# Loads of one chunk moved to another queue, and the first five chunks ordered anew

## The chip, the cores and the metric

The kernel runs on one core of a Trainium2 chip. The metric is device time in microseconds, from runs of the whole program. Five engines work beside each other, each through its own list of instructions in program order: TensorE (PE, matmuls and transposes; its weight loads are listed as PEld), VectorE (DVE), ScalarE (ACT), GpSimd (POOL) and SyncE (SP). They wait for each other by semaphores. Sixteen DMA engines move data. Transfers are put into queues: here SP issues nearly all of them, and GpSimd those of the weights, which are converted from float32 to bfloat16 on the way.

## The reference

Two steps, with B = 4, H = 8 heads, S = 768 positions, D = 64. First attention in which each query sees the first four positions (the sink) and the 128 latest:

```python
scores = scale * np.matmul(q, k.transpose(0, 1, 3, 2))
is_sink = pos[None, :] < n_sink                    # n_sink = 4
rel = pos[:, None] - pos[None, :]
keep = is_sink | ((rel >= 0) & (rel < window))     # window = 128
a = softmax(np.where(keep, scores, -1e9))
attn = np.matmul(a, v)
```

Then its output, as x of 3072 tokens by 512, goes through a feed-forward layer whose hidden layer is the largest of three products:

```python
h = np.maximum(np.maximum(x @ w1, x @ w2), x @ w3)   # 512 x 768 each
out = h @ w_out                                       # 768 x 512
```

## The kernel before

The 3072 tokens are cut into 12 chunks of 256 (`NCH`), three to a batch (`CPB`). Chunks 0 to 5 use one layout, those from `NEW = 6` on another with smaller score tiles. Four pairs of heads (`p` 0 to 3) are worked on at a time; two 64-row heads share the 128 rows of TensorE. For a chunk `ci` the steps are these helpers:

- `load(ci, what)` (lines 93 to 110) issues from SP the DMAs of Q, K and V in float32, 512 KB each, or in two halves of four heads (`part`, 256 KB). A `gate` puts a tiny write into the target tile by GpSimd first, so that SP's DMA waits for GpSimd to get there: `pool_gate` a memset (L603), `after(wi, c)` a copy of one element of weight `wi` (L599), which also waits for that weight to have landed.
- `cast_qk(ci, w, g, eng)` (L118) turns half `g` of Q or K to bfloat16 on the engine named; `cast_v` (L123, or L129 from chunk 6 on) does so for V, `cast_k` (L90) for K from chunk 6 on.
- `turn(ci, w, g, eng)` and `turn2` transpose that half by four matmuls with an identity matrix (L138, L164) into PSUM, and the engine named copies it out (L142, L149, L168, L171). From chunk 4 on `turn_dma` (L182, L188) does it by a transposing DMA that SP issues.
- `premask(ci, pairs)` (L311) writes the additive mask into the score tile by a matmul; `score` (L331; L357 from chunk 6 on) adds the products; `expo` (L398, L374) is the exponential on ScalarE; where there was no `premask`, `mask` (L406, L389) multiplies by a 0/1 mask on VectorE.
- `sink_k(b)` (L283, GpSimd) and `sink_v(b)` (L437, L440) pick the sink's keys and values of batch `b`; `sink_score` (L423, L427) makes their scores.
- `av_open` (L453) takes four PSUM banks and puts the sink's part in; `av(ci, p)` (L471) multiplies with V. A column of ones in V gives the sums; VectorE takes their reciprocal (L476) and scales x by it (L479).
- `xpose(ci, t, eng)` (L491, L493) transposes x into `xT`; from chunk 4 on `xpose_dma` (L498).
- `ffn_h(ci, fp, wi)` (L517) makes 256 hidden columns (block `fp`) with weight `wi`: eight matmuls, then for `wi` 0 a copy by ScalarE (L523), for the others a maximum by VectorE (L527). `ffn_y` (L537) or `y_open`, `y_turn`, `y_out` (L561) make the output, `store` (L589) writes it.

The weights are loaded once, in thirds of 256 columns, by `load_w` (L292), the output weight by `load_wo` (L300), all from GpSimd.

The order of the work is written out by hand: `tc.manual_schedule()` keeps program order on each engine, and the places of the waits follow from the data. PSUM's eight banks are given out from a list, first freed, first taken (`bank`, `give`), when the program is built; so a step takes a fixed bank and waits for whatever used it last. Chunks 0 to 3, with the feed-forward work of chunks 0 to 2 between them, are one long list of calls (lines 629 to 835). A loop follows from `i = 3`: it makes the attention of chunk `i + 1`, the output of chunk `i - 1` and the hidden layer of chunk `i`. Its first turn (with the attention of chunk 4) and its last have an order of their own, the turns between them another.

Around the change the order before is: GpSimd issues the thirds of weight 0, then 1, then 2 (0, 1 and 2 as indices `wi`), while SP loads chunk 2's K and Q behind gates that open when the first weight is there, and its V behind a third gate:

```python
        load(2, 'k', part=0, parts=2, gate=after(0, 300))
        load(2, 'k', part=1, parts=2)
        ...
        load(2, 'q', part=1, parts=2)
        load(2, 'q', part=0, parts=2, gate=pool_gate)
        load_w(2, 0, 256)
        ...
        load(2, 'v', gate=after(0, 300))
```

Of the kernel before, what the change touches and what calls it, by code (L numbers as in the profile page):

```python
# [16 lines left out]
def kernel(  # L17
# [31 lines left out]
    with tc.manual_schedule():  # L49
# [43 lines left out]
        def load(ci, what="kqv", gate=None, part=None, parts=1):  # L93
# [4 lines left out]
            for w in what:  # L98
# [361 lines left out]
        def av(ci, p):  # L460
# [24 lines left out]
        def xpose(ci, t, eng=None):  # L485
# [8 lines left out]
            give(pt)  # L494

# [109 lines left out]
        def cast(ci):  # L605
            if ci >= NCH:
                return
            if ci == NEW:
                for g in range(2):
                    cast_qk(ci, "q", g, nc.gpsimd)  # L610
            for n in range(2):
                for h in range(2):
                    for i in range(2):
                        if ci >= NEW:
                            cast_k(ci, n, h, i, nc.gpsimd)
            if ci < NEW:
                for w in "kq":
                    for g in range(2):
                        cast_qk(ci, w, g, nc.gpsimd)
            if ci == NEW - 1:  # L620
                masks2()
# [6 lines left out]

        load(0, 'q', part=1, parts=2)
        warm(8)  # L630
# [3 lines left out]
        cast_qk(0, 'q', 1, nc.scalar)  # L634
        load(0, 'v', part=1, parts=2)
        masks()
        sink_init()
        factors(msk, addm)
        turn(0, 'q', 1, nc.scalar)
        warm(4)  # L640
        premask(0, (2,))
        cast_qk(0, 'k', 0, nc.scalar)
        cast_qk(0, 'k', 1, nc.vector)
        turn(0, 'k', 1, nc.vector)
        load(1, 'k')
        turn(0, 'k', 0, nc.scalar)
        cast_qk(0, 'q', 0, nc.gpsimd)
        premask(0, (3,))
        score(0, (2,))
        score(0, (3,))  # L650
        turn(0, 'q', 0, nc.vector)
        premask(0, (0,))
        load(1, 'q')
        expo(0, 2)
        cast_v(0, 1, 0, nc.gpsimd)
        cast_v(0, 0, 0, nc.vector)
        cast_v(0, 1, 1, nc.vector)
        cast_v(0, 0, 1, nc.vector)
        load_w(0, 512, 768)
        load(1, 'v')  # L660
        score(0, (0,))
        expo(0, 3)
        cast_qk(1, 'k', 0, nc.gpsimd)
        premask(0, (1,))
        score(0, (1,))
        expo(0, 0)
        expo(0, 1)
        load_w(0, 256, 512)
        av_open(0)
        av(0, 2)  # L670
        av(0, 3)
        turn2(1, 'k', 0, nc.vector)
        cast_qk(1, 'k', 1, nc.scalar)
        av(0, 0)
        cast_qk(1, 'q', 0, nc.gpsimd)
        cast_qk(1, 'q', 1, nc.scalar)
        turn(1, 'k', 1, nc.scalar)
        load_w(0, 0, 256)
        av(0, 1)
        premask(1, (0,))  # L680
        turn2(1, 'q', 0, nc.vector)
        sink_k(0)
        premask(1, (1,))
        turn(1, 'q', 1, nc.scalar)
        cast_v(1, 0, 0, nc.vector)
        cast_v(1, 1, 0, nc.vector)
        load_w(1, 512, 768)
        xpose(0, 0, nc.vector)
        score(1, (0,))
        score(1, (1,))  # L690
        expo(1, 0)
        expo(1, 1)
        load_w(1, 256, 512)
        cast_v(1, 1, 1, nc.gpsimd)
        xpose(0, 1, nc.vector)
        cast_v(1, 0, 1, nc.gpsimd)
        load_w(1, 0, 256)
        score(1, (3,))
        sink_score(1)
        load(2, 'k', part=0, parts=2, gate=after(0, 300))  # L700
        load(2, 'k', part=1, parts=2)
        sink_v(0)
        expo(1, 3)
        ffn_h(0, 2, 0, 1, nc.vector)
        score(1, (2,))
        load(2, 'q', part=1, parts=2)
        load(2, 'q', part=0, parts=2, gate=pool_gate)
        load_w(2, 0, 256)
        expo(1, 2)
        load_w(2, 256, 512)  # L710
        load_w(2, 512, 768)
        mask(1, 3)
        ffn_h(0, 1, 0)
        mask(1, 2)
# [288 lines left out]
```

## Time and profile before

| | |
|---|---|
| time, median of 3 runs | 176.2 us (176.18 to 177.06) |
| profiled execution | 176.05 us, its span 174.3 us |
| TensorE busy | 167.1 us of the span, 96% |
| VectorE, ScalarE, GpSimd busy | 124.6, 89.6, 110.5 us |
| DMA | 34.95 MB, 201 GB/s over the span |

The span runs from the first to the last instruction; the rest of the profiled execution's time lies around it. Rows of the profile read so: line, engine, operation, `target<-source` by the program's names, shapes, `xcount`; in a timeline a row begins with its start and its length in us, and brackets at its end give how long the engine had been idle and what ended that. `w<-in_moe_w_dram` is a weight's DMA, `q_raw`, `k_raw`, `v_raw` are the float32 tiles of Q, K and V. A transfer's time to landing is counted from the start of its issue. Since matmuls are pipelined, a row's length covers more than the time until the next one may start.

### The profile page before, as it was taken

The page shows a single profiled execution, that of the slowest core. Times are in us where ns is not written, and L with a number is a line of the kernel's source. Part 1 is how long each engine was busy: PE and PEld are TensorE (multiplying, and loading weights), DVE is VectorE, ACT ScalarE, POOL GpSimd, SP SyncE. Part 2 cuts the span into 40 slices and gives each one's busy share as a digit, 9 for nine tenths or more (in the row PEclk, how much of TensorE's full clock was granted, in tenths as well). Part 3 has the DMA queues.
Part 4 walks back from the last instruction along what each step waited for, and adds up shares of the span by engine and source line. Part 5 has one row for each costly group of instructions (what it writes and reads, how often), then busy time and mean ns, then how long its engine had stood idle before and what let it go on. Part 6 is the DMA issues. An engine that isn't in the chain of part 4 may idle for free.

```text
span 174.3 us, 5433 instructions
## 1 busy us (share of the span) xinstructions
PE 167.1 (96%) x2228; PEld 129.3 (74%) x2233; DVE 124.6 (71%) x262; ACT 89.6 (51%) x185; POOL 110.5 (63%) x193
## 2 busy tenths in 40 slices
PE   7979999999999999999999999999999999999992
PEld 2446879857696697697797797797797796896871
DVE  3387754796697895886886986877787876776452
ACT  4778535677954813916826617717636516510210
POOL 7399507546489999999999996989998700000000
PEclk9999999999999999999999999999999999999999
DMA  5999999999999999997999999999999415018303
GB/s 148 298 286 197 220 216 258 217 313 271 295 205 302 303 197 224 249 225 202 249 182 252 196 235 240 271 182 213 256 183 289 33 26 162 0 30 154 122 0 120
DMA packets 70505, 34.95 MB, mean 201 GB/s; under 512 B 26448, under 2 KB 68944, under 8 KB 70480
## 3 DMA queue, kind: packets, MB, share of 16 engines
q1 hardware_dynamic: 64784, 31.33, 81.7%
q0 software_dynamic: 5552, 3.15, 12.7%
q8 instruction: 17, 0.28, 0.7%
q10 hardware_dynamic: 144, 0.13, 0.2%
q14 instruction: 8, 0.07, 0.1%
HBM read 25.17 MB, written 6.29 MB: 180 GB/s over the span
## 4 chain that ended last, share of the span: by engine, by line
PE 68%; DMA 18%; POOL 7%; issue 2%; SPq 1%; ACT 1%; DVE 0%; POOLq 0%
PE h_ps L517 43%; PE y_ps L561 11%; DMA k_raw<-in_k_dram 4%; DMA q_raw<-in_q_dram 4%; PE o L471 4%; DMA w<-in_moe_w_dram 4%; PE y_ps L537 4%; PE st L357 3%; DMA v_raw<-in_v_dram 3%; DMA qT<-q_bf 3%; POOL vb L123 3%; POOL w L292 2%; SPq L107 1%; PE st L331 1%; POOL k_bf L118 1%
## 5 line engine op out<-in xcount | busy, mean ns | idle before, releaser
L517 PE MATMUL h_ps<-xT,w 128*128 128x256 bf16 x864 | 101.2, 273 | 0.6 <-DMA w<-in_moe_w_dram 0.4
L517 PEld LDWEIGHTS <-w 128*128 128x128 bf16 x864 | 81.8, 98 | 11.0 <-DMA w<-in_moe_w_dram 0.9
L527 DVE TENSOR_TENSOR h_sb<-h_sb,h_ps 128x512 bf16<-128x512 bf16 (+1 forms) x74 | 49.0, 670 | 17.8 <-PE h_ps L517 16.2
L523 ACT CAST h_sb<-h_ps 128x512 bf16<-128x512 f32 x35 | 20.6, 588 | 51.1 <-PE h_ps L517 51.0
L129 POOL CAST vb<-v_raw 32x512 bf16<-32x512 f32 x48 | 37.5, 781 | 4.0 <-DMA v_raw<-in_v_dram 1.3
L90 POOL CAST k_bf<-k_raw 32x512 bf16<-32x512 f32 x48 | 29.1, 607 | 2.4 <-POOL vb L129 0.4
L398 ACT ACTIVATE e_sb<-st 128x512 bf16<-128x512 f32 (+1 forms) x48 | 23.2, 591 | 1.1 <-PE st L331 1.1
L479 DVE TENSOR_TENSOR x_sb<-o,rc 128x256 bf16<-128x256 f32 x48 | 20.4, 424 | 1.7
L561 PE MATMUL y_ps<-wo,h_sb 64*64 64x512 bf16 (+1 forms) x312 | 21.1, 377 | 0.0
L471 PE MATMUL o<-vb,e_sb 128*128 128x65 bf16 x352 | 16.5, 193 | 0.8 <-DVE vb L123 0.8
L471 PEld LDWEIGHTS <-e_sb 128*128 128x128 bf16 x352 | 14.5, 97 | 3.1 <-ACT e_sb L398 1.0
L123 POOL CAST vb<-v_raw 64x512 bf16<-64x512 f32 x18 | 13.1, 729 | 5.1 <-DMA v_raw<-in_v_dram 4.6
L389 DVE TENSOR_TENSOR e_sb<-e_part,msk 128x1024 bf16<-128x1024 bf16 x16 | 13.4, 862 | 3.1 <-ACT e_part L374 3.0
L406 DVE TENSOR_TENSOR e_sb<-e_sb,msk 128x1024 bf16<-128x1024 bf16 (+1 forms) x18 | 13.1, 751 | 3.4 <-ACT e_sb L398 3.4
L561 PEld LDWEIGHTS <-h_sb 64*64 64x64 bf16 (+1 forms) x312 | 9.9, 106 | 5.0
L374 ACT ACTIVATE e_part<-st 128x384 bf16<-128x384 f32 x32 | 13.1, 496 | 0.5 <-PE st L357 0.5
L537 PE MATMUL y_ps<-wo,h_sb 128*128 128x512 bf16 x49 | 12.6, 380 | 0.3
L476 DVE RECIPROCAL rc<-o 128x4 f32<-128x4 f32 x48 | 8.4, 175 | 4.1 <-PE o L471 4.1
L118 POOL CAST k_bf<-k_raw 128x512 bf16<-128x512 f32 x6 | 3.8, 648 | 9.0 <-DMA k_raw<-in_k_dram 7.5
L118 ACT CAST q_bf<-q_raw 128x512 bf16<-128x512 f32 x13 | 7.6, 621 | 2.7 <-DMA q_raw<-in_q_dram 2.7
L537 PEld LDWEIGHTS <-h_sb 128*128 128x128 bf16 x54 | 4.9, 97 | 5.4 <-DVE h_sb L527 0.5
L427 ACT ACTIVATE e_sink<-sk 128x256 bf16<-128x256 f32 x8 | 3.1, 389 | 10.3 <-PE sk L423 10.3
(90 smaller groups left out, 143.7 us busy)
## 6 DMA issues: line engine op xcount, KB each, us to landing
k_raw<-in_k_dram SPq DMA_DIRECT2D x11, 512.0 KB, 5.8
v_raw<-in_v_dram SPq DMA_DIRECT2D x11, 512.0 KB, 6.7
out_dram<-y_sb SPq DMA_DIRECT2D x11, 512.0 KB, 3.7
q_raw<-in_q_dram SPq DMA_DIRECT2D x10, 512.0 KB, 7.4
w<-in_moe_w_dram POOLq DMA_DIRECT2D x9, 256.0 KB, 6.5
q_raw<-in_q_dram SPq DMA_DIRECT2D x4, 256.0 KB, 7.6
wo<-in_moe_w_out_dram POOLq DMA_DIRECT2D x2, 384.0 KB, 8.2
v_raw<-in_v_dram SPq DMA_DIRECT2D x2, 256.0 KB, 5.1
```

What stands on the lines that cost most here:

```text
L90: f(bfs[ci, "k"][x:x + 32, :, n], raws[ci, "k"][y:y + 32, :, i].rearrange("q (p a) d -> q p a d", a=2))
L123: eng.tensor_copy(vb[ci % RING][64 * i:64 * i + 64, n, :, 0:D], raws[ci, "v"][64 * n:64 * n + 64, :, i])
L129: eng.tensor_copy(vb[ci % RING][x:x + 32, n, :, 0:D], raws[ci, "v"][y:y + 32, :, i])
L389: nc.vector.tensor_mul(x.rearrange("q a (t s) c -> q (a t) s c", t=2), y, msk2)
L398: nc.scalar.activation(e[:, a, lo:], st[a][:, lo:], AF.Exp, scale=scale)
L471: nc.tensor.matmul(o[:, t, a], lhsT=e[:, a, s], rhs=vb[cv % RING][:, n, 2 * p + a], start=first, stop=True, skip_group_check=True)
L479: nc.vector.tensor_mul(xs[ci][:, p], o[:, :, :, 0:D], rc.unsqueeze(3).to_broadcast([128, 2, 2, D]))
L517: nc.tensor.matmul(hp[:, f].rearrange("q (i t r) -> q i t r", i=2, r=x.shape[3]), lhsT=w_sb[wi][:, ds, c0:c0 + 128], rhs=x, start=(ds == 0 ...
L523: (nc.scalar.copy if eng is nc.scalar else eng.tensor_copy)(dst, hp)
L527: nc.vector.tensor_max(dst[:, x], dst[:, x], hp[:, x])
L537: nc.tensor.matmul(yp, lhsT=hs[ci][:, fb, t * 128:(t + 1) * 128], rhs=wo[:, fb], start=(fb == 0), stop=(fb == FB - 1))
L561: nc.tensor.matmul(yps[ci][t][c:c + cols], lhsT=hs[ci][hp, fb, x:x + cols], rhs=wo[hp, fb], start=(turn == 0 and fb == 0), stop=(turn == 1 ...
```

## The change

The six 256 KB halves of chunk 2's Q, K and V are issued by GpSimd (`eng=nc.gpsimd`) and not by SP, without gates, in one queue with the weights: one half of Q behind the whole of weight 0, one half of K and both halves of V behind the whole of weight 1, the rest of Q and K between the thirds of weight 2. The output weight follows at once. Chunk 3's Q has `pool_gate` instead of a gate on weight 2.

The list of chunks 0 to 3 is put into another order, and chunk 4's attention, before the loop's first turn, becomes part of it. All twelve warming matmuls (`warm`) come before the first transposes. Some casts and copies change engines. The masks of chunk 1's pairs that are added beforehand are those of 1 and 2 rather than 0 and 1. `av` gets an engine: for `av(1, 3)`, `av(3, 0)` and `av(3, 1)` four ScalarE instructions do the scaling that was one of VectorE. A new `xpose2` makes both halves of chunk 1's `xT` with the transposes in turns. V of chunk 4 is loaded behind K and Q of chunk 5; of chunk 5's casts three go to ScalarE and one to VectorE. The middle turns of the loop issue what they did.

```diff
-        def load(ci, what="kqv", gate=None, part=None, parts=1):
+        def load(ci, what="kqv", gate=None, part=None, parts=1, eng=None):
...
-                    nc.sync.dma_start(
+                    (eng or nc.sync).dma_start(
...
-        def av(ci, p):
+        def av(ci, p, eng=None):
...
-            nc.vector.tensor_mul(xs[ci][:, p], o[:, :, :, 0:D],
-                                 rc.unsqueeze(3).to_broadcast([128, 2, 2, D]))
+            if eng is nc.scalar:
+                for t in range(2):
+                    for a in range(2):
+                        nc.scalar.activation(xs[ci][:, p, t, a], o[:, t, a, 0:D], AF.Copy,
+                                             scale=rc[:, t, a:a + 1])
+            else:
+                nc.vector.tensor_mul(xs[ci][:, p], o[:, :, :, 0:D],
+                                     rc.unsqueeze(3).to_broadcast([128, 2, 2, D]))
...
+        def xpose2(ci, eng0, eng1):
+
+            xTs[ci] = work.tile([128, DS, 2, 128], BF16, tag="xT", bufs=3, name="xT")
+            pt = [bank([128, DS, 128], BF16, "xt") for t in range(2)]
+            for ds in range(DS):
+                for t in range(2):
+                    nc.tensor.transpose(
+                        pt[t][:, ds], xs[ci][:, ds, t].rearrange("q a d -> q (a d)"), ident)
+            for t, eng in enumerate((eng0, eng1)):
+                (nc.scalar.copy if eng is nc.scalar else eng.tensor_copy)(xTs[ci][:, :, t], pt[t])
+                give(pt[t])
```

The new list, cut to what the prediction speaks of:

```python
        warm(4)
        masks()
        warm(8)
        load(0, 'q', part=1, parts=2)
        cast_qk(0, 'q', 1, nc.scalar)
        turn(0, 'q', 1, nc.scalar)
        premask(0, (2,))
        ...
        cast_qk(0, 'k', 1, nc.vector)
        factors(msk, addm)
        load(1, 'k')
        cast_qk(0, 'k', 0, nc.scalar)
        turn(0, 'k', 0, nc.vector)
        sink_init()
        turn(0, 'k', 1, nc.scalar)
        cast_qk(0, 'q', 0, nc.gpsimd)
        premask(0, (3,))
        turn(0, 'q', 0, nc.vector)
        premask(0, (0,))
        score(0, (2,))
        expo(0, 2)
        ...
        load_w(0, 256, 512)
        premask(1, (1,))
        load(1, 'v')
        load_w(0, 0, 256)
        ...
        load(2, 'q', part=0, parts=2, eng=nc.gpsimd)
        ...
        load_w(1, 512, 768)
        ...
        load_w(1, 256, 512)
        ...
        load_w(1, 0, 256)
        score(1, (3,))
        expo(1, 3)
        cast_v(1, 0, 1, nc.vector)
        load(2, 'k', part=0, parts=2, eng=nc.gpsimd)
        load(2, 'v', part=0, parts=2, eng=nc.gpsimd)
        load(2, 'v', part=1, parts=2, eng=nc.gpsimd)
        load_w(2, 0, 256)
        expo(1, 2)
        load(2, 'q', part=1, parts=2, eng=nc.gpsimd)
        load_w(2, 256, 512)
        load(2, 'k', part=1, parts=2, eng=nc.gpsimd)
        load_w(2, 512, 768)
        load_wo()
        mask(1, 3)
        ffn_h(0, 1, 0)
        av_open(1)
        av(1, 0)
        av(1, 1)
        ffn_h(0, 0, 0)
        av(1, 3, nc.scalar)
        av(1, 2)
        ffn_h(0, 2, 1)
        xpose2(1, nc.scalar, nc.vector)
        cast_qk(2, 'k', 0, nc.scalar)
        cast_qk(2, 'k', 1, nc.gpsimd)
        ffn_h(0, 1, 1)
        ffn_h(1, 0, 0)
        ffn_h(1, 0, 1)
        cast_qk(2, 'q', 0, nc.vector)
        factors(msk0[0], addm0)
        ffn_h(1, 2, 0)
        ffn_h(1, 2, 1)
        ffn_h(1, 1, 0)
        load(3, 'q', gate=pool_gate)
        cast_v(2, 1, 0, nc.gpsimd)
        ...
        turn(2, 'k', 0, nc.scalar)
        ...
        ffn_h(0, 0, 1)
        ffn_h(1, 1, 1)
        ffn_h(0, 0, 2)
        ffn_h(1, 1, 2)
        turn(2, 'q', 1, nc.scalar)
        turn(2, 'q', 0, nc.scalar)
        turn(2, 'k', 1, nc.scalar)
        ...
        ffn_y(0, 1)
        turn(3, 'q', 0, nc.scalar)
        av(2, 1)
        ...
        turn_dma(4, 'q')
        ...
        load(4, 'v')
        ...
        store(0)
        turn_dma(4, 'k')
        mask(3, 3)
        cast_v(4, 1, 0, nc.gpsimd)
        ...
        sink_k(1)
        sink_v(1)
        ...
        cast_qk(5, 'q', 1, nc.scalar)
        cast_qk(5, 'k', 1, nc.scalar)
        sink_score(4)
        store(1)
        turn_dma(5, 'k')
        ...
        store(2)
        av(4, 2)
        ...
        av(4, 0)
        turn_dma(5, 'q')
```

More of the change, by code (lines that the diff above doesn't have):

```diff
@@ L613, in cast @@
                     for i in range(2):
[L614 to L621, printed above, removed]
+                        cast_k(ci, n, h, i, nc.gpsimd)
             if ci > NEW and ci % CPB == 1:
@@ L633 @@
         load(0, 'v', part=0, parts=2, gate=pool_gate)
-        cast_qk(0, 'q', 1, nc.scalar)
         load(0, 'v', part=1, parts=2)
-        masks()
-        sink_init()
[L638 to L646, printed above, removed]
+        cast_qk(0, 'k', 1, nc.vector)
+        factors(msk, addm)
@@ L731 @@
[L731 to L739 removed]
+        ffn_h(1, 0, 0)
+        ffn_h(1, 0, 1)
+        cast_qk(2, 'q', 0, nc.vector)
+        factors(msk0[0], addm0)
+        ffn_h(1, 2, 0)
+        ffn_h(1, 2, 1)
+        ffn_h(1, 1, 0)
+        load(3, 'q', gate=pool_gate)
```

438 lines of the change are left out of this document (199 added, 239 removed).

## The prediction

> **What bounds the kernel now.** I read the windows first (columns: busy us and instruction count of each engine, granted clock, DMA share, GB/s), then the chain that ended last, then the waits of TensorE's weight loads.
>
> ```profile
> 20.00:25.00 5.00, 4.57 (x58) 4.03 (x54) 4.16 (x11) 0.69 (x2) 0.00 (x0) 1.00 1.32 229
> 25.00:30.00 5.00, 5.00 (x52) 4.53 (x51) 1.80 (x3) 3.38 (x6) 3.15 (x6) 1.00 1.27 242
> ...
> 70.00:80.00 10.00, 10.00 (x131) 8.22 (x128) 8.13 (x17) 5.83 (x13) 9.40 (x14) 1.00 0.82 206
> ```
>
> ```profile
> 16.47 6.56 DMA w<-in_moe_w_dram
> ...
> 23.08 3.67 PE h_ps L517 x32
> ...
> 63.38 4.85 DMA qT<-q_bf
> ...
> 68.28 0.29 PE sk L423 x4
> ...
> 76.99 4.37 PE h_ps L517 x40
> ```
>
> ```profile
> PEld L517 <- DMA w<-in_moe_w_dram: 0.6, 1, 0.6
> ...
> PEld L423 <- DMA qT<-q_bf: 0.3, 1, 0.3
> ```
>
> From 23.08 us TensorE is full: 5.00 of 5 us, later 10.00 of 10, at clock 1.00. So the end moves only by what TensorE gains or loses before 23.08 us, or by new holes behind it. Two holes show: 0.6 us of weight loads waiting for the last third of weight 1 (issued at 16.47, landed 23.03), and 0.3 us at 68.28 for chunk 5's transposed Q, of which some 0.1 is the normal step between two matmuls; I count 0.2. That is the whole prize: 0.8 us and crumbs. Eight matmuls of one `ffn_h` call take 4.37/5 = 0.87 us.
>
> What feeds the front is the DMA engines:
>
> ```profile
> 9.00:10.00 1.00, 0.42 (x5) 0.11 (x4) 0.99 (x2) 1.00 (x4) 1.00 (x2) 1.00 1.17 290
> ...
> 14.00:15.00 1.00, 1.00 (x22) 0.64 (x18) 0.99 (x3) 1.00 (x3) 1.00 (x2) 1.00 1.45 195
> ...
> 24.00:25.00 1.00, 1.00 (x12) 0.90 (x10) 0.69 (x1) 0.00 (x0) 0.00 (x0) 1.00 1.31 213
> ```
>
> They move 290 GB/s when only SP's Q, K, V are under way, 195 (counted in the bfloat16 written; twice that is read) when only GpSimd's weights are, 213 when both are. A weight third (256 KB written) alone thus costs 1.34 us of stream, a half of Q, K or V (256 KB) 0.90 us from SP. Over the span, in slices of 4.4 us:
>
> ```profile
> DMA  5999999999999999997999999999999415018303
> ```
>
> They are busy through the first 40 us, so what goes ahead of something delays it.
>
> **The change, part by part.**
>
> *Chunk 2 on GpSimd's queue.* Six halves of 256 KB leave SP and go into the one queue with the weights: q0 behind weight 0; k0, v0, v1 behind weight 1; q1 and k1 amid weight 2.
>
> ```profile
> 13.69 0.79 POOL L292 DMA_DIRECT2D w<-in_moe_w_dram  x1
> ```
>
> ```profile
> w<-in_moe_w_dram POOLq DMA_DIRECT2D x1, 256.0 KB, 6.0
> ```
>
> ```profile
> L292 POOL DMA_DIRECT2D w<-in_moe_w_dram x9: 740/747/1105, 9.3 to 18.9; - x9
> ```
>
> ```profile
> 17.25 0.18 POOL L599 CAST k_raw<-w 1x1 f32<-1x1 bf16 x1
> 17.37 0.09 POOL L603 MEMSET q_raw<- 1x1 f32 x1
> ...
> 26.70 0.61 POOL L118 CAST k_bf<-k_raw 128x512 bf16<-128x512 f32 x1 [6.91 <-DMA k_raw<-in_k_dram]
> ```
>
> Issuing: six times 0.75 us = 4.5 on GpSimd, against 0.4 for the three gates that go (two copies like the 0.18, one memset of 0.09). The 6.91 us in which GpSimd waited before 26.70 take all of it, and the two issues of the output weight now come ahead of the cast instead of behind it; without that idle time the 4.1 us would stand ahead of chunk 2's casts. SP loses five issues and waits for nothing of them. The Trainium skill ("SBUF — State Buffer", section "SBUF: two separate sides") speaks against the move: GpSimd cannot write descriptors while VectorE runs an operation that takes both ports. The nine issues of 740 to 1105 ns bear out 0.36 us at most, so 6 x 0.36 = 2.2 us would still go into the idle time.
>
> Transport: no transfer of plain float32 from GpSimd's queue is in this trace. Upper bound, a half at the weights' written rate: 1.34 us; lower bound, at their read rate (390 GB/s): 0.67. I take SP's 0.90, the same rows of 512 bytes. Weight 1's first third, issued at 13.69, landed 6.0 later at 19.7; with q0 ahead 20.6 (20.4 to 21.0). The second follows 1.34 later, at 21.9. The last third, landed 23.03 before with chunk 2's K on SP beside it, has only q0 ahead: about 23. From there the single queue gives k0 23.9, v0 24.8, v1 25.7, weight 2 first third 27.0, q1 27.9, second third 29.3, k1 30.2, last third 31.5, output weight about 36 (it shares with chunk 3's Q).
>
> *Chunks 0 and 1 anew.*
>
> ```profile
> 3.80 0.72 PE L203 MATMUL warm<-wz 128*128 128x512 bf16 x2
> 4.52 0.40 PE L138 MATMUL pt<-ident,q_bf 128*128 128x128 bf16 x4
> 4.76 0.59 PE L203 MATMUL warm<-wz 128*128 128x512 bf16 x2
> ```
>
> ```profile
> 4.96 0.58 ACT L142 COPY qT<-pt 128x512 bf16<-128x512 bf16 x1 [0.49 <-PE pt L138]
> 5.63 0.62 ACT L118 CAST k_bf<-k_raw 128x512 bf16<-128x512 f32 x1
> 6.77 0.58 ACT L149 COPY kT<-pt 128x512 bf16<-128x512 bf16 x1 [0.52 <-PE pt L138]
> 7.40 3.17 ACT L398 ACTIVATE e_sb<-st 128x384 bf16<-128x384 f32 x8
> ...
> 14.29 2.06 ACT L398 ACTIVATE e_sb<-st 128x512 bf16<-128x512 f32 x4
> 16.22 0.42 ACT L427 ACTIVATE e_sink<-sk 128x256 bf16<-128x256 f32 x1
> 16.48 2.12 ACT L398 ACTIVATE e_sb<-st 128x512 bf16<-128x512 f32 x4
> 18.39 0.69 ACT L523 CAST h_sb<-h_ps 128x512 bf16<-128x512 f32 x1
> ```
>
> ```profile
> 20.29 1.91 PE L517 MATMUL h_ps<-xT,w 128*128 128x256 bf16 x16
> ...
> 22.04 0.61 PE L491 MATMUL xt<-ident,x_sb 128*128 128x128 bf16 x8
> ```
>
> All twelve warming matmuls now stand ahead of the first transposes; the last four go at (0.59 - 0.38) = 0.21 each, so `turn(0,'q',1)` starts 0.7 late, near 5.2. ScalarE copies it at 5.65 to 6.23, and only then casts its half of K (5.63 before), behind which stand both transposes of K, since g = 0 now goes first: cast to 6.85, VectorE's copy to 7.8, ScalarE's to 8.1, first scores 8.25, first exponential 8.6 against 7.40, 1.2 us late. From there ScalarE's list sets the pace: eight exponentials at 3.17/8 = 0.40 to 11.8; copy of K, cast of Q, copy of K, first copy of xT (four of about 0.6, with 0.85 lost waiting for TensorE's banks and GpSimd's Q cast) to 15.0; then 4 x 0.51, 0.26 (16.22 to the next exponential at 16.48), 4 x 0.51 to 19.4; two casts of h to 20.85; and the scalings of `av(1,3)`, four of 128x64. For those no row exists: from 0.1 (the 128x512 start-to-start of 0.51 scaled by columns, no fixed part) to 0.4 (the 128x256 exponential); I take 0.2, being nearer to the 0.26 step. x is whole at 21.65 (21.25 to 22.5).
>
> TensorE meanwhile has the same matmuls. `av_open(1)` waits for `expo(1,3)`, to 18.5; then two `av`, `ffn_h(0,0,0)`, two `av` put `ffn_h(0,2,1)` at 20.55, where its weight lands at 20.6 (20.29 before). It ends 21.45; `xpose2` issues six transposes and waits 0.1 for the last scaling; `ffn_h(0,1,1)` runs 21.9 to 22.8 and covers the copies of xT. At 22.8 everything is done that before was done at 23.08, and the last third of weight 1 is first wanted one `ffn_h` later, at 23.7, when it has landed. Gain 0.3; bounds -0.5 (halves at 0.67, cheap scalings) to +0.7 (scalings 0.4, w late 0.4).
>
> *Chunk 2 and 3.* From 22.8 at 0.87 per call: `ffn_h(1,1,2)` is reached at 30.0 (weight 29.3), `turn(2,'k',1)` at 31.4 (k1 lands 30.2, GpSimd's cast 0.61 more: 30.9). Margins 0.7 and 0.5: no stall. The load of chunk 3's Q now stands behind that cast and two `factors` on GpSimd.
>
> ```profile
> 28.77 0.18 POOL L599 CAST q_raw<-w 1x1 f32<-1x1 bf16 x1
> 29.04 1.07 POOL L238 TENSOR_SCALAR msk<-addm 128x384 bf16<-128x384 bf16 x2
> ...
> 38.14 0.86 POOL L118 CAST q_bf<-q_raw 128x512 bf16<-128x512 f32 x1 [2.32 <-DMA q_raw<-in_q_dram]
> ```
>
> ```profile
> 39.93 0.39 PE L138 MATMUL pt<-ident,q_bf 128*128 128x128 bf16 x4
> ```
>
> Its gate opens at 30.9 + 1.07 = 32.0 instead of 28.95. The bytes ahead of it are the same and the engines have the output weight until then, so it still lands near 38 and is cast by 39.0. TensorE, 0.3 earlier, wants it one `av` (some 0.3) sooner than 39.93, at 39.3. SP's K and V of chunk 3 queue behind it and come no later either. If that cover is gone (output weight done before 32), every microsecond goes to chunk 3.
>
> *Chunks 3 and 4.* V of chunk 4 goes behind chunk 5's Q and K; GpSimd casts it only when landed, and `sink_k(1)` is queued behind that cast.
>
> ```profile
> 54.43 0.28 PE L423 MATMUL sk<-qT,ks 128*32 128x256 bf16 x4
> ```
>
> ```profile
> 45.97 3.45 SPq L182 DMA_TRANSPOSE kT<-k_bf  x2
> ```
>
> ```profile
> kT<-k_bf SPq DMA_TRANSPOSE x1, 5.5
> ```
>
> SP's queue behind Q 3 (through at 37) holds k3, v3, q4, k4, q5, k5 at 1.8 each, the transposed Q 4 (about 0.7) and V 4: it lands near 51, `sink_k(1)` is done 52.8, needed at 54.43 - 0.5 = 53.9. The transposing DMA of K 4 is issued near 47.2 rather than 45.97; 5.5 (first of two) on top is 52.7, the second about 53.6, needed 54. No stall, but half a microsecond to spare. Three casts of chunk 5 go from GpSimd to ScalarE, so `turn_dma(5,'q')` no longer waits for GpSimd's V casts: it is issued behind the store of chunk 2, near 60, and lands by 65, so the 0.2 at 68.28 goes. `av(3,0)` and `av(3,1)` on ScalarE (eight scalings, 1.6) lie beside `ffn_h`. The unrolled loop issues the same instructions.
>
> **Sum**: -0.3 - 0.2 = -0.5. Profiled execution 176.05 (span 174.3 and 1.75 around) gives 175.55; the median 176.2 is 0.15 higher, so I say **175.6**.
>
> **Rivals.**
>
> *A. Plain float32 on GpSimd's queue is slow (1.34 a half).* Ends slower. For it speaks that 195 GB/s is all this queue shows anywhere; against it, that each byte written there is two read. `ffn_h(0,2,1)` waits 0.45, k1 lands 6 x 0.44 = 2.6 later, so `turn(2,'k',1)` waits 1.7, and the output weight costs some 0.4 more: 175.55 + 2.5 = 178.0. It decides from 1.1 us a half.
>
> *B. ScalarE or an in-order queue is short.* Its list is full from 8.6 to 21.7; scalings at 0.4 and 0.3 of extra waits make +0.7 at the front, and the half-microsecond margins at 31.4 and 54 may give 0.5 more: 176.3 to 177.6, middle 176.8.
>
> *C. No effect.* The two queues drain the same bytes and TensorE keeps its pace: 176.1. The Trainium skill ("DMA: Bandwidth & Descriptors", section "Issuing engines are not separate DMA queues") says that the issuing engine only saves sequencer time; the trace agrees: both queues together move 213 GB/s, between the 195 and 290 of each alone.
>
> *D. Halves cheap (0.67) and no margin used up*: 176.05 less all 0.8 of the holes, and 0.1 for crumbs: 175.1. For it speaks the rate at which weights are read; against it, that SP's rows of the same size get 290.
>
> **How the numbers follow.** Forecast 0.42 (own range 175.1 to 176.2), A 0.18, B 0.24, C 0.06, D 0.10. 0.5% is 0.9 us, about what runs of this kernel can tell. Faster (under 175.3): D and the lower edge of the forecast, 0.15. Slower (over 177.1): A and a bit over half of B, 0.31. Same: 0.54. The range 174.9 to 178.0 takes in D, all of B and most of A.
>
> **What would show it.** After: no wait of L517 for `w` near 23; `ffn_h(0,2,1)` starting near 20.6; GpSimd's idle time before its first chunk 2 cast shrunk by 4; L138 of K 2 without a wait near 31; L423 without a wait for qT at 68. Wrong if GpSimd's queue shows under 230 GB/s while only Q, K, V are in it, if ScalarE's first L398 is followed by TensorE holes up to 22, or if TensorE is under 4.9 of 5 us anywhere from 25 to 60.

## The result, and the profile after

The changed kernel takes 178.05 us (median of 20 executions, 176.19 to 181.17), the kernel before beside it on the same chip 176.44 us (20 executions, 175.94 to 177.06): by the medians 1.61 us or 0.9% slower. Five of the 20 executions took 180.0 us or more, with a mean granted clock of 0.988 to 0.990, the other fifteen 178.55 or less with 0.996 to 1.000, and the ratio of 1.0056 (95% interval 1.003 to 1.0082) counts the shorter ones alone. The profiled execution is one of the five: 180.2 us, its span 178.5, clock 0.990. So it shows more than the median's loss.

The waits of TensorE in the changed kernel (us in all, times, longest) begin with one that the kernel before did not have at this length:

```profile
PE sk L423 <- DMA qT<-q_bf: 2.3, 1, 2.3
```

The scores of the sink (L423) come once per chunk that needs them, so their starts serve as milestones. TensorE's timeline after (start, length):

```profile
33.50 0.29 PE L423 MATMUL sk<-qT,ks 128*32 128x256 bf16 x4
...
70.41 0.29 PE L423 MATMUL sk<-qT,ks 128*32 128x256 bf16 x4 [2.27 <-DMA qT<-q_bf]
...
97.34 0.28 PE L423 MATMUL sk<-qT,ks 128*32 128x256 bf16 x4
```

and before, beside the rows at 54.43 and 68.28 in the prediction:

```profile
33.58 0.29 PE L423 MATMUL sk<-qT,ks 128*32 128x256 bf16 x4
...
93.57 0.28 PE L423 MATMUL sk<-qT,ks 128*32 128x256 bf16 x4
```

The last store's issue, by ScalarE's queue, before and after:

```profile
171.49 0.37 ACTq L594 DMA_DIRECT2D out_dram<-y_sb  x1
```

```profile
175.25 0.37 ACTq L612 DMA_DIRECT2D out_dram<-y_sb  x1
```

These give a ledger in which each stretch can be compared. All kernels are read off in the same way; the last three are experiments told below.

| milestone, us | before | after | Q of chunk 5 early | and warming split | and Q's half later |
|---|---|---|---|---|---|
| sink scores, chunk 2 | 33.58 | 33.50 | 33.97 | 33.49 | 33.12 |
| chunk 4 | 54.43 | 54.35 | 54.82 | 54.34 | 53.97 |
| chunk 5 | 68.28 | 70.41 | 68.53 | 68.06 | 67.69 |
| chunk 7 | 93.57 | 97.34 | 93.83 | 93.35 | 92.98 |
| last store's issue | 171.49 | 175.25 | 171.75 | 171.26 | 170.90 |
| end of the span | 174.3 | 178.5 | 175.0 | 174.5 | 174.1 |

From before to after: 0.08 us gained up to chunk 4. From chunk 4 to 5, 16.06 us instead of 13.85: 2.21 lost. From chunk 5 to 7, 26.93 instead of 25.29: 1.64 lost. From there to the last store, 77.91 against 77.92: nothing. Behind it 3.25 instead of 2.8: about 0.4 lost. Together 4.2, the difference of the two spans.

**The 2.21.** SP's list after, up to the transposing DMA that is waited for (V of chunk 5, Q of chunk 6, the store of chunk 1, both transposes of chunk 5's K, V and K of chunk 6, the store of chunk 2, then Q of chunk 5):

```profile
53.50 0.37 SPq L107 DMA_DIRECT2D v_raw<-in_v_dram  x1
53.93 0.58 SPq L107 DMA_DIRECT2D q_raw<-in_q_dram  x1
54.60 1.25 SPq L607 DMA_DIRECT2D out_dram<-y_sb  x1
55.95 3.71 SPq L182 DMA_TRANSPOSE kT<-k_bf  x2
59.76 0.52 SPq L107 DMA_DIRECT2D v_raw<-in_v_dram  x1
60.34 1.48 SPq L107 DMA_DIRECT2D k_raw<-in_k_dram  x1
61.91 0.72 SPq L607 DMA_DIRECT2D out_dram<-y_sb  x1
62.69 2.69 SPq L188 DMA_TRANSPOSE qT<-q_bf  x1
```

The chain that ended last has its landing:

```profile
62.69 7.58 DMA qT<-q_bf
```

From 53.50 on SP's rows follow each other with 0.1 us between them at most: it only issues, and reaches this DMA at 62.69. (Ahead of that, from 51.80 to 53.50, it waits for GpSimd's write that opens the gate of chunk 5's V.) In this stretch it does not stand waiting for VectorE. The copy of y that the store of chunk 2 needs

```profile
60.92 0.68 DVE L557 COPY y_sb<-y_ps 128x512 f32<-128x512 f32 x1
```

ends at 61.60, while SP still issues K of chunk 6 (60.34 and 1.48 make 61.82). The chain puts this store behind VectorE's `h_sb` (L545), but that is a tile which the store does not read. Q lands 7.58 us after the start of its issue, at 70.27; TensorE had come to it at 68.14 (70.41 less 2.27). The kernel before issued it later still, at 63.38, and had it in 4.85 us. Its last load stood seven microseconds ahead, and only the transposes of K between:

```profile
56.20 1.47 SPq L107 DMA_DIRECT2D v_raw<-in_v_dram  x1
57.78 5.51 SPq L182 DMA_TRANSPOSE kT<-k_bf  x2
```

After has 1.5 MB (V, K and the store, 512 KB each) within the three microseconds ahead of it.

**The 1.64.** The windows of after around the hole (busy us and instructions of PE, PEld, DVE, ACT, POOL; granted clock; DMA share; GB/s):

```profile
69.00:70.00 1.00, 0.00 (x0) 0.00 (x0) 0.00 (x0) 0.00 (x0) 0.96 (x2) 1.00 0.11 15
70.00:71.00 1.00, 0.59 (x12) 0.44 (x14) 0.00 (x0) 0.25 (x1) 0.91 (x3) 0.86 1.25 276
71.00:72.00 1.00, 1.00 (x14) 0.65 (x12) 0.00 (x0) 0.85 (x3) 0.96 (x2) 0.50 0.87 132
72.00:73.00 1.00, 1.00 (x8) 0.30 (x4) 0.60 (x1) 1.00 (x3) 0.91 (x3) 0.50 0.76 186
73.00:74.00 1.00, 1.00 (x8) 0.33 (x6) 0.93 (x2) 0.35 (x1) 0.96 (x2) 0.50 1.15 340
74.00:75.00 1.00, 1.00 (x21) 0.79 (x19) 0.32 (x1) 0.47 (x1) 0.94 (x2) 0.93 1.16 307
```

TensorE works again from 70.41, and its clock falls to half behind that: 0.86 in the window from 70 means 0.28 us at half, so from 70.72; 0.93 in the one from 74 means until 74.14. That is 3.42 us at half, worth 1.71 us of work, beside 1.64 lost.

The rest of what the prediction had spoken of, in the timelines and windows of after:

```profile
1.26 5.02 PE L203 MATMUL warm<-wz 128*128 128x512 bf16 x12 [1.26 <-DVE wz L192]
6.12 0.39 PE L138 MATMUL pt<-ident,q_bf 128*128 128x128 bf16 x4
```

```profile
9.50 2.02 ACT L398 ACTIVATE e_sb<-st 128x384 bf16<-128x384 f32 x5 [0.56 <-PE st L331]
...
21.02 0.93 ACT L482 ACTIVATE x_sb<-o,rc 128x64 bf16<-128x64 f32 x4
```

```profile
22.14 5.40 PE L535 MATMUL h_ps<-xT,w 128*128 128x256 bf16 x48
```

```profile
22.00:23.00 1.00, 1.00 (x14) 0.86 (x12) 0.92 (x2) 0.59 (x1) 0.64 (x1) 1.00 1.09 324
...
30.00:40.00 10.00, 10.00 (x114) 7.16 (x112) 7.17 (x11) 7.27 (x15) 6.08 (x13) 1.00 1.12 259
40.00:50.00 10.00, 10.00 (x130) 7.44 (x127) 6.76 (x18) 8.37 (x18) 2.77 (x6) 1.00 1.06 232
50.00:60.00 10.00, 10.00 (x116) 7.44 (x114) 8.77 (x20) 8.54 (x22) 5.43 (x10) 1.00 0.92 266
```

TensorE is full from 22 us to the hole, and the DMA engines move up to 324 GB/s while GpSimd's queue holds plain float32.

### The profile page after: what moved, and what is told of

The parts are those of the page before. It is cut to its first block, busy times and chain, and to the rows that moved or that the text cites. A ratio compares the mean times of both kernels' runs of the same rounds, so it can differ in the third digit from the quotient of the medians.

```text
span 178.5 us, 5446 instructions
## 1 busy us (share of the span) xinstructions
PE 169.5 (95%) x2233; PEld 130.2 (73%) x2233; DVE 126.2 (71%) x262; ACT 93.8 (53%) x200; POOL 110.3 (62%) x190
## 4 chain that ended last, share of the span: by engine, by line
PE 88%; DMA 4%; ACT 4%; DVE 1%; issue 0%; SPq 0%
PE h_ps L535 49%; PE y_ps L579 11%; PE y_ps L555 6%; PE o L471 6%; DMA qT<-q_bf 4%; PE st L331 3%; PE st L357 3%; PE warm L203 3%; ACT e_sb L398 2%; PE pt L138 2%; PE st L311 1%; PE o L453 1%; PE sk L423 1%; PE xt L497 1%; PE y_ps L601 1%
## 5 line engine op out<-in xcount | busy, mean ns | idle before, releaser
L545 DVE TENSOR_TENSOR h_sb<-h_sb,h_ps 128x512 bf16<-128x512 bf16 (+1 forms) x74 | 49.5, 672 | 21.8 <-PE h_ps L535 18.7
L129 POOL CAST vb<-v_raw 32x512 bf16<-32x512 f32 x48 | 36.5, 761 | 3.4 <-DMA v_raw<-in_v_dram 1.2
L90 POOL CAST k_bf<-k_raw 32x512 bf16<-32x512 f32 x48 | 29.9, 622 | 2.6 <-DMA k_raw<-in_k_dram 0.3
L579 PE MATMUL y_ps<-wo,h_sb 64*64 64x512 bf16 (+1 forms) x312 | 22.4, 386 | 0.0
L485 DVE TENSOR_TENSOR x_sb<-o,rc 128x256 bf16<-128x256 f32 x45 | 19.1, 425 | 1.5
L123 POOL CAST vb<-v_raw 64x512 bf16<-64x512 f32 x13 | 9.0, 692 | 11.0 <-DMA v_raw<-in_v_dram 10.5
L118 ACT CAST q_bf<-q_raw 128x512 bf16<-128x512 f32 x14 | 8.2, 621 | 1.5 <-DMA q_raw<-in_q_dram 1.5
L374 ACT ACTIVATE e_sb<-st 128x384 bf16<-128x384 f32 x16 | 6.5, 496 | 2.6 <-PE st L357 2.6
```

The source lines that it names most:

```text
L90: f(bfs[ci, "k"][x:x + 32, :, n], raws[ci, "k"][y:y + 32, :, i].rearrange("q (p a) d -> q p a d", a=2))
L129: eng.tensor_copy(vb[ci % RING][x:x + 32, n, :, 0:D], raws[ci, "v"][y:y + 32, :, i])
L374: nc.scalar.activation(dst, st[a], AF.Exp, scale=scale)
L485: nc.vector.tensor_mul(xs[ci][:, p], o[:, :, :, 0:D], rc.unsqueeze(3).to_broadcast([128, 2, 2, D]))
L545: nc.vector.tensor_max(dst[:, x], dst[:, x], hp[:, x])
L579: nc.tensor.matmul(yps[ci][t][c:c + cols], lhsT=hs[ci][hp, fb, x:x + cols], rhs=wo[hp, fb], start=(turn == 0 and fb == 0), stop=(turn == 1 ...
```

## Experiments

**Q of chunk 5 earlier (e1).** The changed kernel with one line moved in SP's list; all other engines' lists are the same.

```diff
         turn_dma(5, 'k')
+        turn_dma(5, 'q')
         score(4, (0,))
...
         av(4, 0)
-        turn_dma(5, 'q')
```

> The changed kernel with one call moved on SP alone: the transposing DMA of chunk 5's Q stands right behind that of its K (its casts are done by 54.1 us), ahead of the loads of chunk 6's V and K and of the store of chunk 2. Theory 'late Q 5' (all that is lost against the forecast is the wait for this DMA at 68 us and the half-clock time behind it): the wait of L423 for qT is gone, no execution above 177.5, median 175.9 to 176.3, ratio to the kernel before 0.997 to 1.001. Rival 'the front' (twelve warming matmuls and ScalarE's late start cost as well): still 0.5 us or more above the kernel before. Rival 'chance' (the slow executions are of the chip, not of the kernel): the spread of 176 to 181 stays.

176.53 us (before 176.31; ratio 1.0008, 0.9982 to 1.0034). The timeline of SP, then of TensorE:

```profile
59.73 1.39 SPq L188 DMA_TRANSPOSE qT<-q_bf  x1
```

```profile
68.53 0.29 PE L423 MATMUL sk<-qT,ks 128*32 128x256 bf16 x4
```

L423 starts without a wait, and no execution of the twelve has a clock under 0.995 or takes more than 177.53. The median is 0.22 us above the kernel before, a little over the 175.9 to 176.3 that were expected, and the interval does not tell that from nothing; the changed kernel's was 1.61 above. So most of its loss hangs on the place of this one DMA. The gain is still not there: in this profile TensorE is 0.26 behind the kernel before from chunk 7 on, and 0.4 is lost behind the last store.

**The hole filled with matmuls on zeros (e2).** The changed kernel with eleven more matmuls ahead of chunk 5's sink scores (about 2.4 us of work that goes nowhere).

```diff
+            if i == 4:
+                hold(11)
             sink_score(n)
```

> The changed kernel with eleven more matmuls on zeros in front of chunk 5's sink scores, 2.3 us of work in place of the hole, so that TensorE is not idle while it waits for the transposed Q. Theory 'the hole costs twice' (the wait itself, and behind a long one some 3 us at half clock): executions draw together, none above 179, median about 177.5 to 178.3, granted clock 1.00 everywhere. If the clock has nothing to do with the hole, executions above 180 remain.

178.89 us (178.59 to 180.51; ratio 1.0162, 1.0124 to 1.0199). TensorE's timeline, and a window in the former hole:

```profile
69.64 2.54 PE L210 MATMUL warm<-wz 128*128 128x512 bf16 x11
72.38 0.29 PE L430 MATMUL sk<-qT,ks 128*32 128x256 bf16 x4 [0.20 <-DMA qT<-q_bf]
```

```profile
72.00:73.00 1.00, 0.80 (x16) 0.48 (x17) 0.00 (x0) 0.28 (x1) 0.91 (x3) 1.00 1.22 271
```

With the hole's time spent working the clock stays at 1.00 here, and at 0.996 to 1.000 in all six executions. They now all pay for the hole's length: none is below 178.59, and the median is above the 177.5 to 178.3 that were expected. The profile is that of the 180.51, whose clock is 0.999; it is long for another reason. Its chunk 2 milestone stands at 35.17, 1.67 later than in the changed kernel's profile, with waits of TensorE for weights at 18.5 and 22.5 us (0.44 and 0.69). Six executions alone prove little, since 20 of 26 executions of the changed kernel (with e0) keep their clock too; e9 below goes the other way.

**The queue alone (e3).** The kernel before, in its own order, with only the six halves issued by GpSimd and the gates gone.

```diff
-        load(2, 'k', part=0, parts=2, gate=after(0, 300))
-        load(2, 'k', part=1, parts=2)
+        load(2, 'k', part=0, parts=2, eng=nc.gpsimd)
+        load(2, 'k', part=1, parts=2, eng=nc.gpsimd)
...
-        load(2, 'v', gate=after(0, 300))
+        load(2, 'v', parts=2, eng=nc.gpsimd)
```

> The kernel before with chunk 2's halves issued by GpSimd in the kernel before's own order (K, K, Q, Q between weights 1 and 2, V behind weight 2) and without their gates: nothing else. If the queue is what pays (one queue is not slowed by the other, weight 1 lands sooner): the 0.6 us wait for weight 1 shrinks, ratio 0.996 to 0.999. If it costs (V late behind weight 2, Q late): waits at 27 to 33 us and a ratio of 1.003 to 1.01. If the same bytes drain at the same pace: 0.999 to 1.001.

176.31 us (ratio 1.001, 0.999 to 1.003). TensorE, and the last store's issue:

```profile
93.34 0.28 PE L423 MATMUL sk<-qT,ks 128*32 128x256 bf16 x4
```

```profile
171.26 0.37 ACTq L594 DMA_DIRECT2D out_dram<-y_sb  x1
```

TensorE's wait for a weight near 23 is gone and TensorE is 0.1 ahead at chunk 2 (33.48 against 33.58) and 0.23 from chunk 7 to the last store, but the span ends at 174.5, 3.2 us behind the last issue instead of 2.8. The move gives 0.2 on TensorE and takes 0.4 at the end (e10 and e11 show by what). Two of the twelve executions, of 177.20 and 177.26 us, have a mean granted clock of 0.990, though this kernel's profile has no hole at 68; where they lost it no profile shows.

**Chunk 2's loads back on SP, in the new order (e4).** e1 with the loads of chunk 2 where the kernel before had them, behind its gates (its V now ahead of weight 2).

```diff
-        load(2, 'k', part=0, parts=2, eng=nc.gpsimd)
-        load(2, 'v', part=0, parts=2, eng=nc.gpsimd)
...
+        load(2, 'k', part=0, parts=2, gate=after(0, 300))
+        load(2, 'k', part=1, parts=2)
...
+        load(2, 'v', gate=after(0, 300))
```

> The kernel of the first run (Q 5 early) with chunk 2's loads put back on SP, behind the kernel before's gates, all other order as changed. Theory 'the new order needs the new queue': K, Q and V of chunk 2 come in the old order amid weights 1 and 2, weight 1's last third waits again, 0.3 to 1 us slower than the first run. Rival 'the queue is indifferent': within 0.2 us of the first run.

185.41 us (ratio 1.0506, 1.0471 to 1.054). From the chain that ended last, in order of time:

```profile
20.04 16.92 DMA v_raw<-in_v_dram
...
36.99 0.04 DVE vb L123
...
37.45 0.75 DVE h_sb L545 x2
```

V comes at 36.96, last on SP and beside all that GpSimd has issued by then; the new order casts it on VectorE ahead of the maxima of the hidden layer, so these and TensorE behind them stand still. The new order needs V early, and the queue gives it that. This mixes two things (SP's queue, and V behind K and Q on it), so it prices neither. Its six executions have clocks of 0.972 to 0.991; in its profile TensorE waits 2.24 and 3.04 us between 31 and 38.2, and the clock is at 0.50 from 40 to 46.

**Only ahead of the store (e7).** The changed kernel with the DMA one place up in SP's list.

```diff
         av_open(4)
+        turn_dma(5, 'q')
         store(2)
...
         av(4, 0)
-        turn_dma(5, 'q')
```

> The changed kernel with chunk 5's transposing DMA of Q only one place up in SP's list: ahead of the store of chunk 2, still behind the loads of V and K of chunk 6. Theory 'the wait of SP for VectorE's copy of y, with the store's own bytes, makes it late': issued near 61.0 instead of 62.7 it lands about 2 us earlier, near 68, the hole at 68 is 0.5 us or less, TensorE's clock stays at 1.00 behind it, and the time is 176.3 to 177.0. Rival 'the megabyte of V and K of chunk 6 ahead of it on the queue makes it late': it lands at 69.5 or later, the hole stays over 1 us, and the time is 177.5 or more.

176.39 us (176.24 to 176.89; ratio 1.0013, 1.0003 to 1.0024). SP's timeline, and the two landings of Q's transposes between 55 and 75 us (the longer is that of chunk 5):

```profile
60.96 3.13 SPq L188 DMA_TRANSPOSE qT<-q_bf  x1
```

```profile
DMA to landing us min/median/max: 3.2/4.4/5.7
```

Issued 1.73 us earlier it lands 3.6 earlier, at 66.7, still behind V and K of chunk 6, and TensorE does not wait. So the place behind the store is the cause, and the megabyte of V and K alone is borne. The expectation's wait for VectorE is not what the trace of the changed kernel shows (above). Of the 1.73 us 0.78 are the issue of the store itself (61.91 to 62.69), 0.1 an earlier start, and 0.8 the issue of K ahead of it, which takes 0.69 us here and 1.48 in the changed kernel; what lengthened that is open. The 1.9 us less from issue to landing suggest the store's bytes: 512 KB at the 290 GB/s of the window from 63 us in the changed kernel are 1.8 us, an estimate. No run separates them.

**One place later (e9).** The same line moved down, behind the transposing DMA of chunk 4's x.

```diff
-        turn_dma(5, 'q')
         ffn_h(3, 1, 2)
         ffn_h(3, 2, 1)
         xpose_dma(4)
+        turn_dma(5, 'q')
```

> The changed kernel with chunk 5's transposing DMA of Q one place further down in SP's list, behind the transposing DMA of chunk 4's x. Theory 'a hole of over about 2.2 us at 68 us halves TensorE's clock for some 3.5 us behind it': it is issued near 68, lands between 71.5 and 73, the hole is 3 to 4.5 us in every execution, the granted clock is 0.98 to 0.99 in every one of them, the windows behind the hole show 0.5, and the time is 181 to 183.5. Rival 'the clock falls by chance, or because of this chip': the clock is 0.996 to 1.0 in most executions, and the time is 179 to 181.

183.12 us (181.06 to 183.66; ratio 1.0325, 1.0259 to 1.039); the four clocks are 0.978 to 0.991. TensorE's wait and the windows:

```profile
PE sk L423 <- DMA qT<-q_bf: 4.1, 1, 4.1
```

```profile
71.00:72.00 1.00, 0.00 (x0) 0.00 (x0) 0.00 (x0) 0.00 (x0) 0.92 (x2) 0.86 1.00 185
...
77.00:78.00 1.00, 1.00 (x14) 0.68 (x10) 0.00 (x0) 0.78 (x2) 0.90 (x3) 0.50 1.38 260
78.00:79.00 1.00, 1.00 (x9) 0.40 (x6) 0.66 (x1) 1.00 (x3) 0.96 (x2) 0.73 1.04 242
```

Each execution now loses clock. It falls at 71.72, still in the hole, and rises at 78.54 (by the same reckoning as above): 6.82 us, twice the 3.42 of the changed kernel. With the hole certain the lost clock is certain, in four of four, and with the hole filled (e2) it is gone. The 70 executions of the kernels with this DMA earlier (e1, e5, e6, e7, e8) all have 0.995 or more. Together they show that the clock follows the hole, though e3's two executions say that a clock of 0.990 by itself does not prove this hole.

**The changed kernel again (e0).**

> The changed kernel as it stands, beside the others on one chip. Theory 'the hole at 68 us costs its own length, and in some executions the clock behind it as well': the shortest times 176.2 to 177, the longest 180 to 181; a profiled execution on the short side shows the same wait of L423 for qT, of 1 to 2.3 us, with the granted clock at 1.00 behind it or with the wait short. Rival 'the two groups come from something else, such as when the clock rises at the start': the wait of L423 is the same 2.3 us in both.

178.43 us (176.72 to 180.62; ratio 1.0101, 1.0068 to 1.0133), with 0.990 in the one of 180.62 and 0.996 to 1.000 in the others. The profile was again that of the longest: the wait of L423 is 2.5 us, and the clock is at half from 71.04 to 74.46. What the hole measures in the shorter executions therefore stays unseen; their spans of 175.0 to 177.1 leave room for anything from nothing to 2 us.

**Warming split again (e5).** e1 with eight warming matmuls ahead of the first transposes and four behind, as in the kernel before.

```diff
-        warm(4)
-        masks()
         warm(8)
+        masks()
         load(0, 'q', part=1, parts=2)
         cast_qk(0, 'q', 1, nc.scalar)
         turn(0, 'q', 1, nc.scalar)
+        warm(4)
```

> The changed kernel with chunk 5's transposing DMA of Q early (as in e1_q5_early), and of the twelve warming matmuls again eight ahead of the first four transposes and four behind them, as in the kernel before. TensorE's list alone differs from e1_q5_early. Theory 'ScalarE's late start sets the pace of the front': the first transposes start 4.5 to 4.9, the first exponential 0.8 to 1.2 us earlier than with twelve ahead, and the median is 0.3 to 0.8 below e1_q5_early (175.7 to 176.2). Rival 'the weights' queue sets the pace': the first exponential is earlier just the same, but ffn_h(0,2,1) and what follows wait for the weights, and the time is e1_q5_early's (176.5) within 0.2.

176.22 us beside 176.22 (ratio 0.9994, 0.9973 to 1.0014); on another chip:

> e5_warm_split once more, as the neighbour of e8_q0_later on one chip: 176.2, within 0.1% of the kernel before.

176.25 beside 176.27 (0.999, 0.9958 to 1.0022). These intervals overlap that of e1, so the times do not tell the two apart; what follows rests on single profiles. ScalarE's first exponential in e1, then in e5, and TensorE in e5:

```profile
9.98 2.02 ACT L398 ACTIVATE e_sb<-st 128x384 bf16<-128x384 f32 x5 [0.56 <-PE st L331]
```

```profile
8.85 3.17 ACT L398 ACTIVATE e_sb<-st 128x384 bf16<-128x384 f32 x8 [0.56 <-PE st L331]
```

```profile
20.77 1.05 PE L535 MATMUL h_ps<-xT,w 128*128 128x256 bf16 x8 [0.35 <-DMA w<-in_moe_w_dram]
```

ScalarE starts 1.13 us earlier (in both profiles the slow rate of the warming matmuls lasts past 6.5 us); at chunk 2 TensorE is 0.48 ahead (33.49 against 33.97), for a weight now comes too late. In these profiles the warming matmuls did cost, and less than half of what ScalarE lost.

**Half of Q later (e8).** e5 with the half of Q taken from ahead of weight 1 to behind it.

```diff
-        load(2, 'q', part=0, parts=2, eng=nc.gpsimd)
         av(0, 0)
...
+        load(2, 'q', part=0, parts=2, eng=nc.gpsimd)
         load(2, 'k', part=0, parts=2, eng=nc.gpsimd)
```

> e5_warm_split with the load of half 0 of chunk 2's Q behind all of weight 1 instead of ahead of it on GpSimd's queue (next to half 0 of K). Theory 'with the warming matmuls split the front waits for the weights, and Q's half ahead of them is what makes them late': the last and middle thirds of weight 1 land 0.7 to 0.9 us earlier, the wait of L535 for w (0.3 in e5_warm_split) goes, and the median is 0.2 to 0.5 below e5_warm_split's, about 175.9, the first below the kernel before. Rival 'the front is set by ScalarE and TensorE's own list': the wait goes and the time stays at 176.2.

176.01 us beside 176.27 (175.82 to 177.19; ratio 0.9962, 0.9931 to 0.9993). No wait for a weight is left, chunk 2's milestone is 0.46 ahead of before, and of the kernels with more than one execution it is the only one whose interval lies below 1. The 0.26 us are under the 0.5% that the forecast counted as a difference, and the interval overlaps e5's.

**Scalings by VectorE (e6).** e1 with all three `av` scaled by VectorE, as before.

```diff
-        av(1, 3, nc.scalar)
+        av(1, 3)
...
-        av(3, 0, nc.scalar)
-        av(3, 1, nc.scalar)
+        av(3, 0)
+        av(3, 1)
```

> e1_q5_early with the three scalings of x (chunk 1's heads 3, chunk 3's 0 and 1) by VectorE again. Theory 'ScalarE is full to 22 us, VectorE not': x of chunk 1 is whole no earlier or up to 0.4 earlier, nothing else moves, 176.3 to 176.7. Rival 'the scalings on ScalarE cost': four instructions of 0.23 us become one of about 0.3 on VectorE, the time falls by 0.3 to 0.7, to 175.8 to 176.2. Rival 'VectorE is the short one': 0.3 or more slower.

176.60 us (ratio 1.0021, 1.0003 to 1.0038; e1 1.0008), chunk 2's milestone at 33.95 against e1's 33.97: no difference that these times could tell.

**What lengthens the end (e10, e11).** The kernel before with one half, and with all of chunk 2 as three whole loads of 512 KB, on GpSimd's queue.

```diff
-        load(2, 'q', part=0, parts=2, gate=pool_gate)
+        load(2, 'q', part=0, parts=2, eng=nc.gpsimd)
```

> The kernel before with only half 0 of chunk 2's Q on GpSimd's queue: 12 issues there instead of 11 (17 in the changed kernel). What is looked at is the stretch from the last store's issue (ScalarE's queue, L594) to the end of the span: 2.8 us in the kernel before and in e4_sp_loads, 3.2 to 3.3 in every kernel with chunk 2's six halves on GpSimd's queue. Theory 'each plain load on GpSimd's queue lengthens the end of the program': 0.43/6 = 0.07 more, 2.9 us. Rival 'a step once any plain float32 transfer is in that queue': 3.2. Rival 'chance': 2.8 or 3.2 without order.

> e3_queue_alone with chunk 2's K, Q and V on GpSimd's queue as three whole loads of 512 KB instead of six halves: 14 issues there, the same bytes. Theory 'per issue': the stretch from the last store's issue to the end of the span is 3.0 us. Rival 'per byte, or a step': 3.2.

One execution each: 176.32 and 175.89 us (before 176.25), the spans 174.6 and 174.2. Their last store's issues:

```profile
171.63 0.37 ACTq L594 DMA_DIRECT2D out_dram<-y_sb  x1
```

```profile
170.95 0.37 ACTq L594 DMA_DIRECT2D out_dram<-y_sb  x1
```

Behind them lie 3.0 us with one half, 3.25 with three wholes, 3.2 to 3.3 in all kernels with six halves, 2.8 in the two with none (before, e4). "Per issue" falls: three issues cost as much as six. A full step at the first transfer falls as well. The traces show what it is. In each of them the last packet of any DMA ends 1.4 us behind that issue. Then SP closes the program: it waits for the landings of the DMAs, one semaphore after another in a fixed order. Its waits from the last store's landing on are, before, with one half, and after (L998 and L990 are the call of the whole kernel):

```profile
L998 SPq EVENT_SEMAPHORE  x1: 28/28/28, 173.4 to 173.4; - x1
L998 SPq EVENT_SEMAPHORE  x2: 28/28/28, 173.6 to 173.7; - x2
L990 SPq EVENT_SEMAPHORE  x6: 28/28/28, 177.3 to 177.6; - x6
```

(The rows give the lengths in ns, then the first and the last start.) Behind the wait that the last store ends stand none, one, and five more, 0.06 us each. The DMAs of SP and ScalarE get eight semaphores in turn. There are 80 of these DMAs before and in e4, 79 with one half, 75 in all others, so the last store has the eighth, the seventh or the third, and what is behind it in the order is still to be gone through. That is 0.06 of the 0.15 us and 0.3 of the 0.4; the rest is a landing seen 0.1 us later, for which no run gives a reason. All 15 traces fit. So the end hangs on how many DMAs are left to SP, and neither on GpSimd's queue nor on bytes.

## Why the prediction was wrong

It said 175.6 us; the changed kernel takes 178.05. The step that failed is the last of chunks 3 and 4: "it is issued behind the store of chunk 2, near 60, and lands by 65, so the 0.2 at 68.28 goes". Issued at 62.69, landed at 70.27. The prediction gives no working for either figure, and both were too early. It had named the sign itself, L423 without a wait for `qT` at 68.

The issue was taken for a place in SP's list, without adding up what the list issues ahead of it. From 53.50 on these are eight DMAs, 9.1 us without a break. The landing, within 5 us, was priced without what stands ahead of the transfer on the queue. For chunk 4 the prediction had counted SP's loads one by one; here it counted neither V and K of chunk 6 nor the store, and 7.58 us were measured. Either error alone would have been borne: TensorE comes to this Q at 68.14, the row of 4.85 from 62.69 gives 67.54, and 7.58 from 60 gives 67.58. That GpSimd's casts no longer hold this DMA back was right.

The gain itself was there to be had: with the DMA early (e1) TensorE takes 13.71 us from chunk 4 to 5, against 13.85.

The other terms:

- *Sum*: 175.55 and 0.15 for the median make 175.7, not 175.6.
- *Front, -0.3*: -0.08 by the milestones of this one profile. The other profiles with the same front (e0, e1, e7, e9) have chunk 2 at 33.64 to 34.16 and e2 at 35.17, against 33.58 before, so no gain is shown. The twelve warming matmuls all ran at the slow rate in this execution (5.02 us, 0.42 each), where the prediction let the last four run at 0.21, so the first transposes stand at 6.12 and not 5.2, and the first exponential at 9.50 and not 8.6. `ffn_h(0,1,1)` starts at 22.14 (forecast 21.9): most of that lateness was absorbed, as e5 shows from the other side. That ScalarE's list sets the pace of the front was half right: e5 gives it 1.13 us, and 0.48 arrive before a weight sets the pace instead. Putting Q's half ahead of weight 1 is what made that weight late (e8).
- *Halves of plain float32, 0.90 us*: about right; the 324 GB/s in the window from 22 us, with such halves in GpSimd's queue, are 0.81 us a half, the 267 of the next window 0.98. Rival A, whose time of 178.0 lies nearest to the result, fell: e1, with all its loads, takes 176.53. Its number was right for a wrong reason.
- *Scalings, 0.2 each*: 0.23 (21.02, 0.93 for four). e6 shows that their engine does not matter.
- *Chunks 2 and 3, no stall; chunk 4, no stall*: right, TensorE is full from 30 to 60.
- *Issuing hidden on GpSimd*: right, though its idle time came in other places.
- *The end*: the sum had no term for it, and 0.4 us is lost there, 0.3 of it by SP's closing waits (e10, e11). The five issues that SP loses, which the prediction took to be free, are what costs it. Rival C, no effect, is what the move of the queue alone comes to (e3): 0.2 won on TensorE, 0.4 lost behind the last store.
- *Rival B* had the right kind of cause, a list in order, at other places. Its half-microsecond margins at 31.4 and 54 held; the one that failed, at 68, the prediction had put at over 3 us (65 against 68.28).

What no rival held is that a hole costs more than its length. In the profiled execution 2.2 us of waiting took 1.6 more by the clock.

## What to carry to other kernels

A DMA's place in its queue's list is not yet a time. For each transfer that someone needs, go back to the last issue that had to wait, add up the lengths of the issues from there, and add the bytes ahead to the time of landing. When a reordering shaves tenths at the front, do this for each later transfer that it moves, for one hole of 2 us undoes it and can cost nearly as much again through the clock. Where a gain that TensorE's timeline shows does not arrive in the time, look at what stands behind the last store.

## What the runs showed of the hardware

- TensorE's clock can fall to half behind an idle stretch of 2.27 us (after) or 2.50 us (e0). It stays there for 3.42 us in both, and for 6.82, twice that, in e9. The Trainium skill, "TensorE: Matmul & The Clock Gate", section "What's actually happening", says that activity is judged over a free-running window of 3413 ns. The durations agree with it. The Trainium skill, "TensorE: Matmul & The Clock Gate", section "Why this matters for your kernels", warns of idle gaps over some 3 us; here less was enough in two profiled executions. By the clock it happened in 6 of 26 executions of the changed kernel; how long TensorE idled in the other 20 was not seen.
- The start is not the same in each execution. In the kernel before the slow rate of the warming matmuls ended near 4.5 us (the twelve take 4.3 us in all), in the profiles of after and e1 only behind the last of the twelve, at 6.3 and 6.6. The granted clock reads 1.00 in these windows, so it does not show this rate. Chunk 2's milestone differs as well between profiles whose lists differ only later, 33.50 in after, 33.97 in e1, 35.17 in e2, and not by the slow rate alone: e2's ended early, near 5.5. So 0.5 us at the front between two single profiles need not be the edit's. The comparison of e1 with e5 rests on two profiles of like starts.
- In the changed kernel the time from issue to landing of a transposing DMA ranged from 3.2 to 7.6 us; the longest stood behind 1.5 MB on its queue.
- SP's closing waits take 0.06 us each, and how many stand behind the last landing depends on the number of DMAs issued by SP and ScalarE: none with 80, one with 79, five with 75.
